# Band attention and two MLP layers on one core: the fourth f tile joins the banks of the first three, and batches 2 and 3 come first in the block products

## The chip, the core and the metric

The kernel runs on one core of a Trainium2 chip, in one launch. Its engines are TensorE (PE in the profile; PEld is its weight load), VectorE (DVE), ScalarE (ACT), GpSimd (POOL) and SyncE (SP), which here only issues DMAs. The metric is device time in microseconds, the median of several executions. One execution was profiled; all rows below come from it.

## What is computed

The reference, cut to what matters: attention over 4 batches, 8 heads, 512 local and 32 global tokens with 64 elements a head; then two MLP layers (512 to 2048 to 512) over all 2304 tokens.

```python
x = attn_out.transpose(0, 2, 1, 3).reshape(B * S, H * D)   # 2304 x 512
h = x @ w_in                                               # layer 0, 2048 wide
g = np.where(h > 0, h, np.exp(np.minimum(h, 0)) - 1)
x = g @ w_out
h = x @ w_in2                                              # layer 1
g = np.where(h >= 1, h, np.where(h <= -1, 0, (h + 1) ** 2 / 4))
return g @ w_out2
```

## The kernel before, in words

**Numbers.** Every fp32 operand of the MLP is held as two parts, high and low (`xh`, `xl`; `gh`, `gl`; a weight's two halves), and a product is three matmuls: low weight by high x, high by low, high by high. Weights arrive as 64-bit words in a `wraw` tile (two buffers) and are split by `decode`, which takes eight steps on DVE and two on ACT, most of them 128x1024.

**The two layers.** The hidden width of a layer is 16 f tiles of 128. The tokens are four batches j of 512 local tokens, plus one group of global rows. For an f tile and a batch, `up` makes 12 matmuls of 128x512 into one PSUM bank, ACT and DVE apply the function and split the result, and `down` makes 12 matmuls into four banks (dn0 to dn3, one for each 128 of the output). When the last f tile of a group is added, `collect` evicts each bank with ACT into an `ev` tile, which a DMA takes to `sums` in DRAM: a plain store by SP for the group that has f = 0, an accumulating DMA by POOL for the others. The `ev` tile is free again when that DMA is through. A `rows` item does the same for the global rows.

**Plain f tiles.** In layer 0 the f tiles 0 to 3 are done that way ("plain"): `PLAIN = [[0, 1, 2], [3]]`. The first three go over batches 0, 1, 2, 3 and are evicted. The fourth, whose weights `decode_one` brings, follows over batches 2, 3, 0, 1 as a group of its own, with its own evictions and its own `rows` item; its downs spread into what comes next.

**Block products.** All other f tiles go in 14 pairs by Strassen-Winograd blocks. A pair and a duo of batches (duo 0 is batches 0 and 1, duo 1 is 2 and 3) make seven products of 6 matmuls (`quad`, `product`), in place of the 8 blocks of plain products. Each takes a form of x (X11, X21, X22, T1 to T4). Forms are made by `first_forms` for layer 0 (and `later_forms` for layer 1), stored to `forms` in DRAM, and held in the tiles that had the tokens (`PLACES`). When the groups switch from one duo to the other, `product` issues two loads of 512 KB for each form once its last reader is under way (`load_form`). In the first group, duo 0, the three X forms stand where batches 0 and 1 have their tokens; the four T forms, made in spare tiles of `w_ps[0]` and stored, are loaded into the tiles of batches 2 and 3.

**What sets the order.** Code is written in events; after each event `pop` may emit one waiting down, and `step` advances the jobs in `line` (`decode_in`, `decode_out`, `first_forms`, ...), which `job_at` starts at an event number. A scheduler then orders the instructions of each engine by what is ready. Every engine works its own list in order. PE, for instance, can't pass a matmul that waits.

## Time and profile before

| | |
|---|---|
| median of 3 runs | 852.78 us (851.49 to 853.75) |
| the profiled execution | 852.66 us, span 850.9 us |
| granted TensorE clock, mean | 0.991 |
| PE busy | 814.0 us, 96% of the span |
| DVE busy | 685.6 us, 81% |
| ACT busy | 554.3 us, 65% |
| POOL busy | 102.3 us, 12% |
| DMA | 180.88 MB |

PE is nearly always at work, so the table alone says little; time is lost where a window of PE is not full. The attention ends about 115 to 128 us into the span, the plain f tiles and the first block products fill 120 to 260 us, and the switch from layer 0 to layer 1 lies around 460 to 540 us. In a window row the columns are busy microseconds of PE, PEld, DVE, ACT and POOL, then the granted clock as a share of the full one, the mean busy share of the 16 DMA engines, and GB/s.

### The profile page before, as it was taken

How to read it: one execution, taken by the hardware profiler on the slowest of the kernel's cores; microseconds unless marked ns; L12 is line 12 of the kernel's file. 1: busy time of each engine (PE TensorE's matmuls, PEld its weight loads, DVE VectorE, ACT ScalarE, POOL GpSimd, SP SyncE). 2: the span in 40 equal slices, each digit the busy share in tenths (PEclk: the TensorE clock that was granted, in tenths of full speed). 3: DMA queues.
4: the chain of work that ended last, by engine and by line, in shares of the span. 5: the costliest groups of instructions: out<-in, count | busy, mean ns of one | idle time of the engine just before them, and what ended most of it. 6: DMA issues, size and time to landing. Idle time of an engine off the chain costs nothing.

```text
span 850.9 us, 15914 instructions
## 1 busy us (share of the span) xinstructions
PE 814.0 (96%) x6058; PEld 662.6 (78%) x6058; DVE 685.6 (81%) x1279; ACT 554.3 (65%) x948; POOL 102.3 (12%) x162
## 2 busy tenths in 40 slices
PE   8799999998979999999999988999999999999998
PEld 5676778886758888888888866788888888888886
DVE  5798889968869979786789899998988598945463
ACT  5788765855746667555656366878867686867451
POOL 2231300002213022201100000000020111111000
PEclk9999999999999999999999999999999999999999
DMA  8988729997999189538916846437853795369523
GB/s 268 318 262 275 255 85 373 370 392 213 298 328 160 43 245 318 115 65 211 313 69 247 297 187 259 148 99 250 294 119 79 198 323 123 49 142 302 200 101 110
DMA packets 67132, 180.88 MB, mean 213 GB/s; under 512 B 9328, under 2 KB 9584, under 8 KB 65904
## 3 DMA queue, kind: packets, MB, share of 16 engines
q1 hardware_dynamic: 55248, 158.62, 53.8%
q0 software_dynamic: 11520, 20.98, 15.3%
q8 instruction: 48, 0.79, 0.4%
q10 hardware_dynamic: 288, 0.26, 0.1%
q14 instruction: 28, 0.23, 0.1%
HBM read 116.65 MB, written 63.18 MB: 211 GB/s over the span
## 4 chain that ended last, share of the span: by engine, by line
PE 76%; DMA 11%; DVE 7%; ACT 5%; issue 2%; POOL 0%; SPq 0%; ACTq 0%; DVEq 0%; POOLq 0%
PE dn L368 34%; PE up L1054 26%; DMA wraw<-in_w 5%; PE up L281 3%; PE dn L381 2%; DMA xh<-form 2%; PE s L146 2%; PE up L293 2%; DMA k_sb<-in_kT 1%; PE pt L146 1%; DMA sum<-ev 1%; PE up L146 1%; PE po L146 1%; ACT sn L146 1%; DVE xl L861 1%
## 5 line engine op out<-in xcount | busy, mean ns | idle before, releaser
L1054 PE MATMUL up<-xh,wi 128*128 128x512 f32 x784 | 264.5, 397 | 12.8 <-DMA xh<-form 3.9
L368 PE MATMUL dn<-gh,wo 128*128 128x512 f32 x608 | 184.6, 391 | 3.7 <-ACT ev L347 3.4
L1054 PEld LDWEIGHTS up<-xh,wi 128*128 128x128 f32 x784 | 149.9, 191 | 47.6 <-DVE u L861 4.9
L861 DVE TENSOR_TENSOR u<-up,u 128x512 f32<-128x512 f32 x196 | 131.7, 686 | 51.4 <-PE up L1054 43.2
L1054 PE MATMUL up<-xl,wi 128*128 128x512 f32 x392 | 155.0, 395 | 0.0
L352 POOL DMA_DIRECT2D sum<-ev x80 | 72.7, 1118 | 593.8 <-ACT ev L347 588.9
L368 PEld LDWEIGHTS dn<-gh,wo 128*128 128x128 f32 x608 | 113.5, 188 | 29.2 <-ACT ev L347 5.5
L368 PE MATMUL dn<-gl,wo 128*128 128x512 f32 x304 | 114.4, 390 | 0.4 <-DVE gl L334 0.4
L330 ACT ACTIVATE gh<-g 128x512 fp32r<-128x512 f32 x123 | 77.1, 628 | 53.1 <-DVE g L313 20.0
L334 DVE TENSOR_TENSOR gl<-g,gh 128x512 fp32r<-128x512 f32 x123 | 84.0, 686 | 13.0 <-ACT gh L330 11.8
L1054 PEld LDWEIGHTS up<-xl,wi 128*128 128x128 f32 x392 | 75.0, 191 | 14.9
L347 ACT ACTIVATE ev<-dn 128x512 f32<-128x512 f32 x110 | 61.7, 597 | 34.2 <-PE dn L368 19.6
L306 ACT ACTIVATE g<-u,half_sb 128x512 f32<-128x512 f32 x64 | 45.8, 720 | 48.2 <-DVE u L861 40.0
L368 PEld LDWEIGHTS dn<-gl,wo 128*128 128x128 f32 x304 | 57.0, 188 | 12.8 <-DVE gl L334 0.9
L368 PE MATMUL dn<-gh,xl 128*128 128x512 f32 x160 | 62.2, 392 | 2.6 <-ACT gh L330 2.5
L368 PE MATMUL dn<-gh,xh 128*128 128x512 f32 x160 | 62.3, 389 | 0.0
L315 DVE TENSOR_TENSOR g<-u,g 128x512 f32<-128x512 f32 x64 | 43.8, 686 | 20.9 <-ACT g L308 20.9
L368 PE MATMUL dn<-gl,xh 128*128 128x512 f32 x160 | 58.4, 389 | 0.0
L307 ACT ACTIVATE g<-g,one_sb 128x512 f32<-128x512 f32 x68 | 48.7, 720 | 1.4
L301 ACT ACTIVATE g<-u 128x512 f32<-128x512 f32 x48 | 30.1, 630 | 26.1 <-DVE u L861 22.4
L303 ACT ACTIVATE g<-g,one_sb 128x512 f32<-128x512 f32 (+1 forms) x64 | 45.6, 714 | 1.5
L308 ACT ACTIVATE g<-g 128x512 f32<-128x512 f32 x68 | 42.5, 627 | 1.1
(189 smaller groups left out, 1357.3 us busy)
## 6 DMA issues: line engine op xcount, KB each, us to landing
wraw<-in_w SPq DMA_DIRECT2D x56, 512.0 KB, 6.6
xh<-form SPq DMA_DIRECT2D x46, 512.0 KB, 9.6
xl<-form SPq DMA_DIRECT2D x46, 512.0 KB, 8.1
sum<-ev POOLq DMA_DIRECT2D x80, 256.0 KB, 8.4
v_sb<-in_vwin SPq DMA_DIRECT2D x64, 260.0 KB, 4.6
form<-xh SPq DMA_DIRECT2D x20, 512.0 KB, 4.6
form<-xl SPq DMA_DIRECT2D x20, 512.0 KB, 4.3
sum<-ev SPq DMA_DIRECT2D x32, 256.0 KB, 5.4
```

The source lines that it names most:

```text
L146: return lambda *args, **kw: tc.keep_in_program_order(fn(*args, **kw))
L303: eng.scalar.activation(self.g, self.g, AF.Relu, bias=one_sb, scale=-1.0)
L306: eng.scalar.activation(self.g, self.ps, AF.Relu, bias=half_sb, scale=-0.5)
L307: eng.scalar.activation(self.g, self.g, AF.Relu, bias=one_sb, scale=-1.0)
L315: eng.vector.tensor_tensor(g, self.ps, g, ALU.max)
L330: eng.scalar.activation(self.gh, self.g, AF.Copy)
L334: eng.vector.tensor_tensor(self.gl, self.g, self.gh.bitcast(F32), ALU.subtract)
L347: eng.scalar.activation(out, ps, AF.Copy)
L352: eng.gpsimd.dma_start(to, out, accum_op=ALU.add)
L368: eng.tensor.matmul(banks[d], w[:, d * P:(d + 1) * P], g, start=first and k == 0, stop=last and k == 2)
L861: return eng.vector.tensor_tensor(out, a, b, op)
L1054: eng.tensor.matmul(ps, w[:, a, col + k * P:col + (k + 1) * P], x[b][:, k * SL:(k + 1) * SL], start=k + t == 0, stop=k == 1 and t == 2,)
```

## The change

Five things are changed, and one follows from them.

1. All four plain f tiles form one group. Per batch they add into the same four banks, which are evicted once, through SP. The `rows` item is one as well.
2. The first block group is duo 1 (batches 2 and 3), and the order of the duos in all later groups is mirrored. `PLACES` is mirrored too.
3. `first_forms(1)` makes the T forms straight into the tiles of batches 0 and 1, after the last up product that reads them ((0, 3, 1) is born). The eight loads of T forms before the first group fall away.
4. `decode_in(0)` starts at event 3 (was 5), `first_forms(1)` at 5 (was 3), `decode_in(1)` at 8 (was 10), `decode_out(0)` at 10 (was 8).
5. `decode_out` turns its three places by one: pair 0's output weights go into the token tile (3, 0), which is free when batch 3's last up product is done.
6. At the end of layer 0 the first two sums (not the last two) use the spare tile.

Counted in the order of the program: PE 4782 instructions before and after; ACT 952 and 933; DVE 1281 and 1278; POOL 167 and 151 (accumulating DMAs 80 and 64); SP 375 and 367.

```diff
-PLAIN = [[0, 1, 2], [3]]
+EARLY, LATE = [0, 1, 2], 3
+PLAIN = EARLY + [LATE]
...
@@ decode_in(n)
         yield
+        while n == 2 and len(w_ps) < 2:
+            yield
         w = w_ps[n % 3 // 2].tile([P, 2, 8 * BLOCK], F32R, tag=f"wi{n % 3}", name="wi")
...
@@ decode_out(n)
-        i = (n + 1) % 3
+        i = (n + 2) % 3
...
-        while len(w_ps) < 2:
+        while n in (1, 2) and len(w_ps) < 2 or n == 0 and (0, LATE, 3) not in born:
             yield
...
-            w = [token_tile(1, 0, part) for part in range(2)]
+            w = [token_tile(3, 0, part) for part in range(2)]
...
-    PLACES = {X11: (0, 0), X21: (0, 1), X22: (1, 1), T2: (2, 0), T3: (2, 1), T1: (3, 0), T4: (3, 1)}
+    PLACES = {X11: (2, 0), X21: (2, 1), X22: (3, 1), T2: (0, 0), T3: (0, 1), T1: (1, 0), T4: (1, 1)}
...
@@ first_forms(duo)
-        for i, j, h in ((X11, j0, 0), (X21, j0, 1), (X22, j1, 1)):
-            keep([flat(x[j][h]) for x in (xh, xl)], (0, duo, i), last_low[0])
+        if duo == 0:
+            for i, j, h in ((X11, j0, 0), (X21, j0, 1), (X22, j1, 1)):
+                keep([flat(x[j][h]) for x in (xh, xl)], (0, duo, i), last_low[0])
...
+        while duo and (0, LATE, 1) not in born:
+            yield
         for i, pair in enumerate((((T2, x22), (T3, x12)), ((T1, x11), (T4, x21)))):
-
-            t = w_ps[0].tile([P, 2, 2, 2 * SL], F32R, tag=f"wi{i}", name="form")
+            if duo == 0:
+
+                t = w_ps[0].tile([P, 2, 2, 2 * SL], F32R, tag=f"wi{i}", name="form")
             for k, (form, src) in enumerate(pair):
-                split([t[:, k, part] for part in range(2)], src)
-                keep([t[:, k, part] for part in range(2)], (0, duo, form))
+                out = new_form(form) if duo else [t[:, k, part] for part in range(2)]
+                last_split[0] = split(out, src)
+                if duo:
+                    holds[form] = 0, 1
+                keep(out, (0, duo, form))
...
@@ pop()
-                if layer == 0 and j >= 2:
-                    if j == 2:
+                if layer == 0 and j < 2:
+                    if j == 0:
...
-    job_at(3, first_forms(1), False)
-    job_at(5, decode_in(0))
-    job_at(8, decode_out(0))
-    job_at(10, decode_in(1))
-    for i, js in enumerate(((0, 1, 2, 3), (2, 3, 0, 1))):
-        fs = PLAIN[i]
...
+    job_at(3, decode_in(0))
+    job_at(5, first_forms(1), False)
+    job_at(8, decode_in(1))
+    job_at(10, decode_out(0))
+    for j in range(B):
+        for f in PLAIN:
+            ds = range(KT // 2, KT) if j == 0 and f in EARLY else range(KT)
+            downs.append(["down", 0, PLAIN, j, f, ds])
...
+    begin, item = rows(0, PLAIN, [(0, 0), (0, LATE)])
+    downs.append(item)
+    ups = [(f, j) for j in range(B) for f in PLAIN if (0, f, j) not in born]
+    for f, j in ups[1:2] + ups[0:1] + ups[2:]:
+        need(lambda: (0, f) in w_in)
+        event(lambda: plain(0, f, j))
...
-    need(lambda: all((0, duo, i) in made_forms for duo in range(2) for i in range(7)))
-    for i in (T2, T3, T1, T4):
-        load_form(0, 0, i)
...
-    for c, duos in enumerate(((0, 1), (1, 0), (0, 1), (0, 1), (1, 0), (0, 1), (1, 0))):
+    for c, duos in enumerate(((1, 0), (0, 1), (1, 0), (1, 0), (0, 1), (1, 0), (0, 1))):
```

How the order moves, at three places. First PE. Before, the downs of the fourth f tile (`wo_3083`) stand among the block products (`wi_3382`), into banks of their own, dn_3609 and the next:

```order
L1054 MATMUL up_3831<-xh_3755,wi_3382 128x512
L368 MATMUL dn_3609<-gh_3449,wo_3083 128x512 x2
L368 MATMUL dn_3609<-gl_3451,wo_3083 128x512
L1054 MATMUL up_3839<-xh_3759,wi_3382 128x512
L1054 MATMUL up_3839<-xl_3760,wi_3382 128x512
L1054 MATMUL up_3839<-xh_3759,wi_3382 128x512 x2
L1054 MATMUL up_3839<-xl_3760,wi_3382 128x512
L1054 MATMUL up_3839<-xh_3759,wi_3382 128x512
L368 MATMUL dn_3616<-gh_3449,wo_3083 128x512 x2
L368 MATMUL dn_3616<-gl_3451,wo_3083 128x512
L368 MATMUL dn_3623<-gh_3449,wo_3083 128x512 x2
L368 MATMUL dn_3623<-gl_3451,wo_3083 128x512
```

After, at the place where batch 0's first three f tiles end, some up products (`up_3325`), then the fourth tile's downs (`wo_3077`) into the banks dn_2979 to dn_3073 that batch 0 had, and then batch 1's first (dn_3216):

```order
L282 MATMUL up_3325<-xl_94,wh0_143 128x512
L282 MATMUL up_3325<-xh_92,wh0_143 128x512
L369 MATMUL dn_2979<-gh_3114,wo_3077 128x512 x2
L369 MATMUL dn_2983<-gh_3114,wo_3077 128x512 x2
L369 MATMUL dn_3069<-gh_3114,wo_3077 128x512 x2
L369 MATMUL dn_3073<-gh_3114,wo_3077 128x512 x2
L369 MATMUL dn_2979<-gl_3116,wo_3077 128x512
L369 MATMUL dn_2983<-gl_3116,wo_3077 128x512
L369 MATMUL dn_3069<-gl_3116,wo_3077 128x512
L369 MATMUL dn_3073<-gl_3116,wo_3077 128x512
L369 MATMUL dn_3216<-gh_2476,wl0_144 128x512
L369 MATMUL dn_3216<-gh_2476,wh0_143 128x512
```

The downs of the fourth tile have moved out of the block products to the end of each batch, and the next batch's downs follow them directly.

Second DVE, around the decode of the second pair's up weights. Before, `wi_3689` comes behind the output weights of the first pair (`wo_3576`):

```order
L239 SCALAR_TENSOR_TENSOR wo_3576<-rest_3578,wraw_3485 128x1024
L216 TENSOR_SCALAR rest_3691<-wraw_3637 128x1024
L220 SCALAR_TENSOR_TENSOR rest_3691<-wraw_3637,rest_3691 128x1024
L228 TENSOR_SCALAR top_3690<-top_3690 128x1024
L232 TENSOR_SCALAR top_3690<-top_3690 128x1024
L233 SCALAR_TENSOR_TENSOR top_3690<-wraw_3637,top_3690 128x1024
L238 TENSOR_SCALAR wraw_3637<-top_3690 128x1024
L239 SCALAR_TENSOR_TENSOR wi_3689<-rest_3691,wraw_3637 128x1024
L861 TENSOR_TENSOR whole_3746<-wi_3689 128x1024
L861 TENSOR_TENSOR mixed_3747<-whole_3746 128x256 x2
L861 TENSOR_TENSOR mixed_3747<-mixed_3747,whole_3746 128x256
L861 TENSOR_TENSOR mixed_3747<-whole_3746,mixed_3747 128x256
```

After, the second pair's weights are `wi_3557`:

```order
L240 SCALAR_TENSOR_TENSOR wi_3557<-rest_3559,wraw_3517 128x1024
L335 TENSOR_TENSOR gl_3515<-g_3509,gh_3513 128x512
L314 SCALAR_TENSOR_TENSOR g_3549<-up_3536,g_3549 128x512
L862 TENSOR_TENSOR whole_3602<-wi_3557 128x1024
L335 TENSOR_TENSOR gl_3555<-g_3549,gh_3553 128x512
L862 TENSOR_TENSOR mixed_3603<-whole_3602 128x256 x2
L314 SCALAR_TENSOR_TENSOR g_3594<-up_3581,g_3594 128x512
L862 TENSOR_TENSOR mixed_3603<-mixed_3603,whole_3602 128x256
L862 TENSOR_TENSOR mixed_3603<-whole_3602,mixed_3603 128x256
L335 TENSOR_TENSOR gl_3600<-g_3594,gh_3598 128x512
L862 TENSOR_TENSOR wi_3557<-mixed_3603,wi_3557 128x1024
L217 TENSOR_SCALAR rest_3658<-wraw_3611 128x1024
```

They stand among the last plain f tiles' work (`g`, `gl`), and the output weights of the first pair (xl_3656) come behind them.

Third SP, between the attention and the first block products. Before (`form_0_*` and `form_1_*` are the forms of duo 0 and 1 of layer 0, `wraw` weights):

```order
L958 DMA form_1_3_125<-form 128x1024
L1027 DMA xh<-form_0_2_117 128x1024
L958 DMA form_1_5_127<-form 128x1024
L958 DMA form_1_3_125<-form 128x1024
L1027 DMA xl<-form_0_2_117 128x1024
L1027 DMA xh<-form_0_4_119 128x1024
L1027 DMA xl<-form_0_4_119 128x1024
L958 DMA form_1_5_127<-form 128x1024
L350 DMA sum_2_109<-ev 128x512 x2
L867 DMA wraw<-in_w 128x512
L350 DMA sum_2_109<-ev 128x512 x2
L867 DMA wraw<-in_w 128x512
```

After:

```order
L961 DMA form_1_1_123<-xl 128x1024
L961 DMA form_1_5_127<-xl 128x1024
L868 DMA wraw<-in_w 128x512 x2
L961 DMA form_1_6_128<-xh 128x1024
L961 DMA form_1_6_128<-xl 128x1024
L868 DMA wraw<-in_w 128x512 x2
L351 DMA sum_3_110<-ev 128x512 x4
L868 DMA wraw<-in_w 128x512 x2
L1037 DMA xl<-form_0_0_115 128x1024
L1037 DMA xh<-form_0_0_115 128x1024
L1037 DMA xl<-form_0_1_116 128x1024
L1037 DMA xh<-form_0_1_116 128x1024
```

The loads `xh<-form` and `xl<-form` ahead of the weights are gone; the first ones now belong to the first switch of duos.

## Rows read from the trace of the kernel before

**Rows 1.** The page, busy time, share of the span and instructions of each engine

```profile
PE 814.0 (96%) x6058; PEld 662.6 (78%) x6058; DVE 685.6 (81%) x1279; ACT 554.3 (65%) x948; POOL 102.3 (12%) x162
```

**Rows 2.** Windows: width, busy PE, PEld, DVE, ACT, POOL, clock, DMA share, GB/s

```profile
120.00:140.00 20.00, 19.87 (x148) 15.77 (x148) 18.14 (x26) 10.61 (x20) 0.00 (x0) 1.00 0.57 216
140.00:160.00 20.00, 20.00 (x90) 16.57 (x89) 19.18 (x23) 14.79 (x25) 0.00 (x0) 1.00 1.01 380
160.00:180.00 20.00, 20.00 (x94) 16.87 (x93) 17.97 (x25) 13.86 (x21) 0.00 (x0) 1.00 1.02 391
180.00:200.00 20.00, 20.00 (x96) 16.66 (x95) 12.66 (x19) 12.00 (x21) 0.00 (x0) 1.00 0.87 328
200.00:220.00 20.00, 15.16 (x57) 11.19 (x56) 16.66 (x23) 11.47 (x19) 7.88 (x8) 0.91 0.89 224
220.00:240.00 20.00, 16.11 (x81) 13.21 (x80) 18.97 (x29) 14.58 (x23) 6.05 (x7) 0.97 1.08 307
240.00:260.00 20.00, 18.68 (x76) 14.70 (x75) 12.67 (x19) 9.88 (x17) 4.82 (x5) 0.94 0.96 279
260.00:280.00 20.00, 20.00 (x91) 16.48 (x91) 19.96 (x30) 13.12 (x20) 3.54 (x4) 1.00 0.89 188
```

**Rows 3.** Timeline of PE, 200 to 262 us: start, length, instruction, [idle before, its releaser]

```profile
202.28 0.72 PE L368 MATMUL dn<-gh,wo 128*128 128x512 f32 x2 [1.22 <-ACT ev L347]
...
203.08 0.62 PE L368 MATMUL dn<-gh,wo 128*128 128x512 f32 x2
...
203.77 0.62 PE L368 MATMUL dn<-gh,wo 128*128 128x512 f32 x2
...
208.22 0.80 PE L1054 MATMUL up<-xh,wi 128*128 128x512 f32 x1 [2.90 <-DVE wi L239]
...
211.72 0.62 PE L1054 MATMUL up<-xh,wi 128*128 128x512 f32 x2
...
215.57 0.73 PE L368 MATMUL dn<-gh,wo 128*128 128x512 f32 x2 [0.72 <-ACT ev L347]
...
239.36 0.77 PE L1054 MATMUL up<-xh,wi 128*128 128x512 f32 x1 [3.89 <-DMA xh<-form]
...
242.06 0.76 PE L368 MATMUL dn<-gh,wo 128*128 128x512 f32 x2
...
249.02 0.50 PE L368 MATMUL dn<-gh,xl 128*128 128x512 f32 x1 [0.49 <-ACT gh L330]
...
254.90 0.73 PE L368 MATMUL dn<-gh,wo 128*128 128x512 f32 x2 [0.82 <-ACT ev L347]
```

**Rows 4.** Windows of 2 us, the same columns

```profile
208.00:210.00 2.00, 1.78 (x4) 1.50 (x5) 1.86 (x4) 0.45 (x1) 0.00 (x0) 0.55 1.10 196
...
240.00:242.00 2.00, 2.00 (x6) 1.58 (x5) 1.86 (x3) 0.61 (x2) 0.86 (x1) 0.50 1.06 293
```

**Rows 5.** The chain of waits from 195 to 262 us: start, length, what

```profile
204.93 9.92 DMA sum<-ev
...
221.02 18.21 DMA xh<-form
```

**Rows 6.** Timeline of DVE: the fourth f tile's weights, the second pair's up weights

```profile
130.32 1.23 DVE L239 SCALAR_TENSOR_TENSOR wo<-rest,wraw 128x1024 fp32r<-128x1024 uint32 x1
...
206.94 1.22 DVE L239 SCALAR_TENSOR_TENSOR wi<-rest,wraw 128x1024 fp32r<-128x1024 uint32 x1
```

**Rows 7.** DMA issues of 200 to 262 us: count, KB each, median us to landing

```profile
sum<-ev POOLq DMA_DIRECT2D x20, 256.0 KB, 8.6
...
xh<-form SPq DMA_DIRECT2D x7, 512.0 KB, 17.6
```

**Rows 8.** DMA issues of 128 to 200 us

```profile
xh<-form SPq DMA_DIRECT2D x4, 512.0 KB, 8.1
```

**Rows 9.** Groups of ACT's instructions from 124 to 280 us: busy, mean ns, idle before

```profile
L347 ACT ACTIVATE ev<-dn 128x512 f32<-128x512 f32 x38 | 21.7, 598 | 17.1 <-DMA sum<-ev 7.6 <-PE dn L368 7.4 <-PE up L1054 1.9
```

**Rows 10.** A window of 20 us at the layer switch, columns as in group 2

```profile
500.00:520.00 20.00, 16.93 (x70) 13.35 (x71) 20.00 (x26) 11.55 (x16) 0.00 (x0) 0.83 0.46 184
```

**Rows 11.** Timeline of SP at the layer switch

```profile
474.85 15.98 SPq L867 DMA_DIRECT2D wraw<-in_w  x4
```

More of the change, by code (lines that the diff above doesn't have):

```diff
@@ L40 @@
 NB = B + 1
-PLAIN = [[0, 1, 2], [3]]
+EARLY, LATE = [0, 1, 2], 3
+PLAIN = EARLY + [LATE]
 WCOLS = KT * P + DM
-W_EARLY = len(PLAIN[0])
+W_EARLY = len(EARLY)
 UP_EARLY = 5
@@ L186, in band_attention_then_two_mlps @@
     rows_in[0, 0] = lambda k, part: early[part][:, :, k * P:(k + 1) * P]
-    for f in PLAIN[0]:
+    for f in EARLY:
         w_in[0, f] = [w[:, f, 0:KT * P] for w in early]
@@ L753, in early_ups @@
         def early_ups():
-            for f, j in [(f, j) for j in range(B) for f in PLAIN[0]][:UP_EARLY]:
+            for f, j in [(f, j) for j in range(B) for f in EARLY][:UP_EARLY]:
                 u = Up(0, f, j)
@@ L836, in band_attention_then_two_mlps @@
                 ps_dn.append(mpool("ps_dn0", 1, space=PSUM))
-                for f in PLAIN[0]:
-                    down(0, PLAIN[0], 0, f, first, range(KT // 2))
+                for f in EARLY:
+                    down(0, PLAIN, 0, f, first, range(KT // 2))
         for _ in weights:
@@ L878, in decode_one @@
             pass
-        rows_in[0, 1] = lambda k, part: w[:, part, k * P:(k + 1) * P].rearrange("p (f c) -> p f c", f=1)
+        rows_in[0, LATE] = lambda k, part: w[:, part, k * P:(k + 1) * P].rearrange("p (f c) -> p f c", f=1)
         w_in[0, f] = [w[:, i, 0:KT * P] for i in range(2)]
@@ L1034, in band_attention_then_two_mlps @@
     banks = {0: first}
-    born = {(0, f, j): -LAG for f, j in [(f, j) for j in range(B) for f in PLAIN[0]][:UP_EARLY]}
+    born = {(0, f, j): -LAG for f, j in [(f, j) for j in range(B) for f in EARLY][:UP_EARLY]}
     made_forms, holds, summed, w_out_uses = set(), {}, {}, {}
@@ L1199, in event @@
             pop()
+        if len(w_ps) < 2 and not any(PLAIN in item for item in downs):
+            w_ctx.close()
+            w_ps.append(mpool("w_third", 1))
         for fn in soon.pop(now[0], []):
@@ L1212, in job_at @@
         due.setdefault(n, []).append((job, ahead))
-    job_at(0, decode_one(PLAIN[1][0]))
+    job_at(0, decode_one(LATE))
     job_at(1, first_forms(0), False)
-    job_at(3, first_forms(1), False)
-    job_at(5, decode_in(0))
-    job_at(8, decode_out(0))
-    job_at(10, decode_in(1))
-    for i, js in enumerate(((0, 1, 2, 3), (2, 3, 0, 1))):
-        fs = PLAIN[i]
-        for j in js:
-            for f in fs:
-                ds = range(KT // 2, KT) if i + j == 0 else range(KT)
-                downs.append(["down", 0, fs, j, f, ds])
-        begin, item = rows(0, fs, [(0, i)])
-        downs.append(item)
-        for j in js:
-            for f in fs:
-                if (0, f, j) not in born:
-                    if i:
-                        need(lambda: (0, f) in w_in)
-                    event(lambda: plain(0, f, j))
-            if len(w_ps) < 2 and i:
-                while downs[0][2 if downs[0][0] == "down" else 4] == PLAIN[0]:
-                    pop()
-                w_ctx.close()
-                w_ps.append(mpool("w_third", 1))
-        event(begin)
@@ L1241, in band_attention_then_two_mlps @@
-    for i, (j, h) in ((X11, (0, 0)), (X21, (0, 1)), (X22, (1, 1))):
+    job_at(3, decode_in(0))
[6 more added lines that the diff above has]
+            downs.append(["down", 0, PLAIN, j, f, ds])
+    last_split = [None]
+    begin, item = rows(0, PLAIN, [(0, 0), (0, LATE)])
+    downs.append(item)
+    ups = [(f, j) for j in range(B) for f in PLAIN if (0, f, j) not in born]
@@ L1242, in band_attention_then_two_mlps @@
+    for f, j in ups[1:2] + ups[0:1] + ups[2:]:
+        need(lambda: (0, f) in w_in)
+        event(lambda: plain(0, f, j))
+        if ready():
+            pop()
+    event(begin)
+    for i, (j, h) in ((X11, (2, 0)), (X21, (2, 1)), (X22, (3, 1))):
         slot[i] = [flat(x[j][h]) for x in (xh, xl)]
-        holds[i] = 0, 0
-    need(lambda: all((0, duo, i) in made_forms for duo in range(2) for i in range(7)))
-    for i in (T2, T3, T1, T4):
-        load_form(0, 0, i)
+        holds[i] = 0, 1
+        keep(slot[i], (0, 1, i), last_split[0])
@@ L1257, in band_attention_then_two_mlps @@
             if c == 3:
-                job_at(at + 2, later_forms(1), False)
+                job_at(at + 2, later_forms(0), False)
             job_at(at + 5 + late, decode_in(2 * c + 2))
@@ L1261, in band_attention_then_two_mlps @@
             if c == 2:
-                job_at(at + 9, later_forms(0), False)
+                job_at(at + 9, later_forms(1), False)
             job_at(at + 12 + late // 3, decode_in(2 * c + 3))
```

## The prediction

> **What bounds the kernel now.** I read the page first: TensorE (PE) is busy in 814.0 of the span's 850.9 us [rows 1], so only time that PE loses can be won, and the question is where it loses. The windows of 20 us answer it: from 120 to 200 us, and again from 260 us on, PE is at 19.87 to 20.00 of 20; it falls to 15.16, 16.11 and 18.68 between 200 and 260 [rows 2]. That is the stretch in which the fourth f tile, called [3] here, and the first block products run, and it is what the diff rewrites. PE's own timeline there shows six holes: 1.22, 2.90, 0.72, 3.89, 0.49 and 0.82 us, together 10.04 [rows 3]; the reader should look at the bracket behind each row, which names what ended the hole. After the two longest, the granted clock is at its half level (0.55 and 0.50 in the windows of 2 us) [rows 4]. What that costs comes from the spacing: at the full level three matmuls take 203.77 − 203.08 = 0.69 us, 0.23 each; from 208.22 to 211.72 stand 8 matmuls where 8 × 0.23 = 1.84 would do (1.66 lost), from 239.36 to 242.06 stand 6 where 1.38 would do (1.32 lost) [rows 3]. So the stretch loses 10.04 + 2.98 = 13.0 us. The causes, hole by hole:
>
> - 1.22, 0.72 and 0.82 us end with an eviction on ACT. The chain of waits shows why the second is late: an accumulating DMA of POOL is in flight for 9.92 us from 204.93 on, and the next eviction needs its `ev` tile back [rows 5]. These are the evictions of [3] and of the first blocks' downs.
> - 2.90 us ends with the DVE instruction that writes `wi` of the second pair (206.94, 1.22 us long) [rows 6]. DVE was not slow, it was given decode_in(1) last of all.
> - 3.89 us ends with the load of a form: issued at 221.02, landed 18.21 us later [rows 5].
> - 0.49 us ends with an ACT copy; I leave it where it is.
>
> **The change part by part.**
>
> *One set of evictions.* 16 of 38 ACT evictions of the stretch 124 to 280 us [rows 9] and 16 accumulating DMAs of POOL fall away, since [3] adds into the banks of the first three. Their ACT time (16 × 0.598 = 9.6 us) and DMA time lie beside PE; on the path stood only the holes of 1.22 and 0.72 us, at [3]'s banks. Both go: −1.94. The 0.82 us hole is at a group that stays; I count half: −0.4.
>
> *The same matmuls, in another place.* No matmul is added or dropped (4782 before and after in the program's order). PE's work until the end of the first block products is the same, so the end of the plain stage moves by what it waits, not by what it does. Moved in front: 12 up and 12 down matmuls per batch of [3], whose weights DVE finishes at 131.55 (130.32 and 1.23 us) [rows 6]; PE comes to them at about 132.1, counted in matmuls of 0.23 us from 120 us on, so no wait there; were the decode late, the nearest hole of that kind, 2.90, bounds the price.
>
> *A new wait.* All downs of a batch now end on the same four banks, and the next batch's first down follows at once on PE (the order shows dn_3216 right behind the last of dn_2979 to dn_3073). It waits for the evictions, which on ACT can sit behind one 128x1024 `top` that itself waits for a weight load. Behind the waiting matmul PE's queue is in order, so nothing passes it. The trace of before has no such row at this place; bounds from the nearest: 0 (before, the same handover between batches inside [0, 1, 2] cost nothing: PE 20.00 in 160 to 200 [rows 2]) and the 2.90 of [rows 3] with its 1.66 for the clock. I take +0.6 for the first handover and +0.8 for the three others together, since ACT has 4 evictions of 0.598 us and PE needs the first bank after one of them.
>
> *decode_in(0) and decode_in(1) earlier, decode_out(0) later.* The order puts wi_3557 (second pair) ahead of the first block products. Walking DVE's queue with the durations of the trace from 131.5 us, it is done at about 192, while PE comes to the second pair at about 204: 12 us of room, and the hole of 2.90 with its 1.66 goes: −4.56. In exchange decode_out(0) goes behind it, into tile (3,0), which is free only after the last up product of batch 3; by the same walk it is written at 203 to 205 and its first reader stands on PE at about 206. Nothing covers a slip there; price 0 to 2.90, taken +0.5.
>
> *Forms of duo 1 straight into tiles.* Eight loads of 512 KB are gone and eight stores read from the token tiles instead of `form` tiles; the 8 split operations on DVE and ACT are the same. They wait for (0, 3, 1) to be born, about 140 us; behind them on DVE stands decode_in(1), which has the 12 us above. SP's queue keeps the stores in the same stretch, where the DMA share is already 1.01 to 1.02 without a loss on PE (20.00) [rows 2].
>
> *The first switch of duos.* The X11 load of before took 18.21 us because it shared the DMA engines with the accumulates: in 200 to 262 us the median of a load of `xh` is 17.6 us beside 20 POOL transfers, while in 128 to 200 us, without them, it is 8.1 [rows 7, 8]. After the change, the load of X11 is issued at about 205 and T3's at about 218 by the walk, needed at 221 and 234.5; POOL's first accumulate comes at about 240. With some 7 MB to move at the 307 GB/s of 220 to 240 us [rows 2] the last lands near 226: some 8 us to spare, so the 3.89 and its 1.32 go: −5.21. If the loads still took 18.21 us, T3's would land at 236.2, 1.7 late.
>
> *The rest.* In the groups behind, the two duos change names and the order stays. The switch of layers at 480 to 540 us (PE 16.93 in 500 to 520 at a clock of 0.83 [rows 10]) is mirrored, with a few stores in other places: ±3 by the size of one hole there, taken 0.
>
> Sum against the profiled execution, 852.66 us (span 850.9 and 1.8 around it; the median of the runs, 852.78, is 0.12 away): 852.66 − 1.94 − 0.4 − 4.56 − 5.21 + 0.6 + 0.8 + 0.5 = 842.45. Taking the 0.49 too would give 842.0. I say **842.4**.
>
> **The rivals.**
>
> *B, DVE becomes the bound.* DVE is busy 18.14 + 19.18 + 17.97 + 12.66 + 16.66 + 18.97 + 12.67 = 116.25 of the 140 us from 120 to 260 [rows 2]. With 12 us taken out, the same work must fit into 128, a share of 0.91. For it: the room is small. Against it: from 260 to 280 DVE is at 19.96 of 20 while PE is at 20.00, so a full DVE does not by itself stop PE. If DVE's waits for PE and ACT hold it at 0.88, it takes 132.1 us, 4 more: 846.5.
>
> *C, one set of banks.* Each handover of banks idles as the 1.22 us hole does, in all four batches, 4.9 us instead of the 1.4 taken, and the clock falls once more (+1.3): 847.2. For it: the new wait above. Against it: before, the same kind of handover left PE at 20.00.
>
> The Trainium skill (TensorE: Matmul & The Clock Gate, section "A second HAM failure mode: psum-queue depth-cycling") reports a kernel whose cycling through PSUM banks gives short idles between groups of matmuls, and a clock that swings between its levels. That is this rival's rule, and it speaks against the change; by the trace of before (clock 1.00 in 160 to 200 us over two such handovers) it does not act here so far.
>
> *D, the loads at the first switch are still late.* Nothing of the 5.21 is won: 847.7.
>
> *E, slower.* At the switch of layers SP spends 15.98 us on issuing four weight loads, at 474.85, because their buffers come free late [rows 11]; the `sums` loads and the form stores ahead of them change places. If the weights of the first pair of layer 1 slip by as much again behind the new stores, with layer 0's products already used up on PE, that is +16: 858.4. It decides once the slip is over the 10 us that the earlier part gained; below that the kernel is still faster.
>
> *F, the gain is not there.* The plain stage's end is not set by what I named, and the time won before 260 is waited away at the next late operand: 852.7.
>
> **How the numbers follow.** Forecast 0.58; B 0.16; C 0.08; D 0.08; E 0.04; F 0.06. The likeliest gives 842.4, with 839 to 845.5 by its own bounds (nothing lost at the handovers, 0.49 and the whole 0.82 won: 840; less 1 from the layer switch; the upper ends of the new waits: +3). B, C and D end at 847.7, so the range goes from 838.8 to 848.2; E and F lie outside. A measurement of this kernel can tell 0.3% (2.6 us) from no change: faster than 850.2 is all of the forecast, B, C and D and a little of F, 0.88; within, 0.07; slower, 0.05.
>
> **What would show it.** Right: in the trace after, no hole over 1 us on PE between 200 and 250 us, no half-level window there, the chain of waits without a form load in it, no POOL accumulate before about 235 us. Right for the new wait: `dn` rows with a short idle behind "ACT ev" near 148 us. Wrong: DVE at 20.00 in every window from 200 to 260 with PE waiting for `u` or `gl` (B); a row of idle at every batch's first `dn` (C); a load of X11 or T3 ending a hole (D); the windows 480 to 540 much below 17 (E).

## The result and the profile after

The changed kernel takes 840.08 us (median of 4 runs, 838.48 to 840.94), against 852.13 us for the kernel before on the same chip; the ratio is 0.9855 with a 95% interval of 0.9832 to 0.9878, so 12 us or 1.4% faster. The forecast was 842.4 us, with a range of 838.8 to 848.2. The profiled execution took 840.41 us, its span is 838.6 us.

The windows of 20 us, with the columns of [rows 2] (width, busy PE, PEld, DVE, ACT, POOL, granted clock, DMA share, GB/s):

```profile
140.00:160.00 20.00, 19.99 (x88) 16.26 (x87) 20.00 (x26) 15.76 (x24) 0.00 (x0) 1.00 0.89 327
160.00:180.00 20.00, 20.00 (x90) 16.55 (x89) 18.49 (x23) 12.60 (x18) 0.00 (x0) 1.00 0.65 242
180.00:200.00 20.00, 20.00 (x98) 17.03 (x97) 15.96 (x22) 10.56 (x18) 0.00 (x0) 1.00 1.02 359
200.00:220.00 20.00, 20.00 (x92) 16.54 (x91) 18.82 (x26) 13.48 (x21) 0.00 (x0) 1.00 0.80 265
220.00:240.00 20.00, 20.00 (x101) 17.03 (x100) 19.21 (x31) 11.79 (x18) 0.00 (x0) 1.00 0.93 343
240.00:260.00 20.00, 19.99 (x90) 16.21 (x90) 17.98 (x25) 14.61 (x23) 7.63 (x8) 1.00 0.77 130
```

PE had 15.16, 16.11 and 18.68 busy us in the three windows from 200 to 260 us [rows 2]; it now has 20.00, 20.00 and 19.99, and the clock stays at 1.00. PE's timeline lists no hole from 130 to 470 us, where before it listed the six of [rows 3]. POOL, which began its accumulating transfers at 202.55 us, now begins at 242.97:

```profile
242.97 3.74 POOL L353 DMA_DIRECT2D sum<-ev  x4 [133.19 <-ACT ev L348]
```

The loads of forms, 17.6 us in the median in 200 to 262 us before [rows 7], take 8.0. The issues of that stretch after (count, KB, median us to landing):

```profile
wraw<-in_w SPq DMA_DIRECT2D x8, 512.0 KB, 6.5
xl<-form SPq DMA_DIRECT2D x7, 512.0 KB, 7.1
xh<-form SPq DMA_DIRECT2D x7, 512.0 KB, 8.0
sum<-ev POOLq DMA_DIRECT2D x8, 256.0 KB, 6.9
```

The switch of layers is not better. PE's holes there, in the timeline after:

```profile
477.60 0.47 PE L369 MATMUL dn<-gh,xl 128*128 128x512 f32 x1 [1.10 <-DVE sums L356]
...
489.43 0.58 PE L294 MATMUL up<-wi,xh 128*128 128x256 f32 x1 [3.62 <-DVE u L862]
...
508.98 0.74 PE L369 MATMUL dn<-gh,wo 128*128 128x512 f32 x2 [1.21 <-DVE wo L240]
```

From 440 to 540 us PE idled 8.74 us before (busy 91.26 of 100); in the 100 us from 428 on it now idles 9.46 (busy 90.54). The granted clock is 0.97 over these 100 us in both, so half-level stretches cost some 3 us in each (an estimate from the clock).

**How runs are compared below.** All programs here have the same list of PE instructions up to the last transposes of the attention (`ot`), yet the time of that row differs from profile to profile:

```profile
130.00 0.60 PE L147 MATMUL ot<-eye_sb,o_sb 128*128 128x128 f32 x4
```

```profile
126.33 0.60 PE L147 MATMUL ot<-eye_sb,o_sb 128*128 128x128 f32 x4
```

These are the changed kernel and one of the experiments (i_scalar_q); the kernel before stands at 127.67, and b_in1_first at 130.79. So up to 4.5 us of a total come from a stage that no edit touches. Each kernel has one profile, so whether such a difference belongs to the kernel or to the run is not shown. I therefore also give the length from that row to the end of the span: 850.9 − 127.67 = 723.2 us before, 838.6 − 130.00 = 708.6 after. By that measure the change is worth 14.6 us; the medians say 12.

### The profile page after: what moved, and what is told of

Its sections match the earlier page's. It is cut to its first block, busy times and chain, and to the rows that moved or that the text cites. A ratio compares the mean times of both kernels' runs of the same rounds, so it can differ in the third digit from the quotient of the medians.

```text
span 838.6 us, 15816 instructions
## 1 busy us (share of the span) xinstructions
PE 809.2 (96%) x6058; PEld 661.8 (79%) x6058; DVE 685.6 (82%) x1276; ACT 547.4 (65%) x929; POOL 87.6 (10%) x146
## 4 chain that ended last, share of the span: by engine, by line
PE 83%; DVE 7%; DMA 4%; ACT 3%; issue 3%; SPq 0%; DVEq 0%
PE dn L369 38%; PE up L1064 28%; PE up L282 4%; PE up L294 3%; DMA wraw<-in_w 3%; PE dn L382 2%; PE s L147 2%; PE up L147 1%; PE po L147 1%; DVE u L862 1%; PE pt L147 1%; DVE xl L862 1%; ACT sn L147 1%; ACT pT L147 1%; PE ot L147 1%
## 5 line engine op out<-in xcount | busy, mean ns | idle before, releaser
L1064 PE MATMUL up<-xh,wi 128*128 128x512 f32 x784 | 258.6, 391 | 1.8 <-DVE u L862 1.0
L369 PE MATMUL dn<-gh,wo 128*128 128x512 f32 x608 | 180.4, 390 | 2.9 <-ACT gh L331 1.7
L1064 PEld LDWEIGHTS up<-xh,wi 128*128 128x128 f32 x784 | 147.3, 188 | 33.8 <-DVE u L862 1.9
L1064 PE MATMUL up<-xl,wi 128*128 128x512 f32 x392 | 152.7, 389 | 0.0
L353 POOL DMA_DIRECT2D sum<-ev x64 | 58.4, 1250 | 594.6 <-ACT ev L348 593.7
L369 PE MATMUL dn<-gl,wo 128*128 128x512 f32 x304 | 110.7, 389 | 0.0
L369 PEld LDWEIGHTS dn<-gl,wo 128*128 128x128 f32 x304 | 57.1, 188 | 11.9
L348 ACT ACTIVATE ev<-dn 128x512 f32<-128x512 f32 x96 | 53.4, 599 | 19.3 <-PE dn L369 18.0
L316 DVE TENSOR_TENSOR g<-u,g 128x512 f32<-128x512 f32 x64 | 43.6, 685 | 14.6 <-ACT g L309 14.5
L302 ACT ACTIVATE g<-u 128x512 f32<-128x512 f32 x48 | 30.2, 629 | 35.8 <-DVE u L862 29.4
L308 ACT ACTIVATE g<-g,one_sb 128x512 f32<-128x512 f32 x68 | 48.7, 721 | 1.3
L304 ACT ACTIVATE g<-g,one_sb 128x512 f32<-128x512 f32 x63 | 45.5, 723 | 1.5
```

Of the source, the lines that this page charges most:

```text
L304: eng.scalar.activation(self.g, self.g, AF.Relu, bias=one_sb, scale=-1.0)
L308: eng.scalar.activation(self.g, self.g, AF.Relu, bias=one_sb, scale=-1.0)
L316: eng.vector.tensor_tensor(g, self.ps, g, ALU.max)
L348: eng.scalar.activation(out, ps, AF.Copy)
L353: eng.gpsimd.dma_start(to, out, accum_op=ALU.add)
L369: eng.tensor.matmul(banks[d], w[:, d * P:(d + 1) * P], g, start=first and k == 0, stop=last and k == 2)
```

## The experiments

Each kernel is told with its edit, what was expected, and what came. "Length" is from the `ot` row to the end. The theory at the start was the prediction's: six holes with causes of their own, of which one is the late decode. Its rivals were that the mirrored duos with their saved loads are the gain, or that the accumulating transfers are behind all of it.

**m_old_duos: one set of banks, but batches 0 and 1 first.**

```diff
-    PLACES = {X11: (2, 0), X21: (2, 1), X22: (3, 1), T2: (0, 0), T3: (0, 1), T1: (1, 0), T4: (1, 1)}
+    PLACES = {X11: (0, 0), X21: (0, 1), X22: (1, 1), T2: (2, 0), T3: (2, 1), T1: (3, 0), T4: (3, 1)}
...
+    need(lambda: all((0, duo, i) in made_forms for duo in range(2) for i in range(7)))
+    for i in (T2, T3, T1, T4):
+        load_form(0, 0, i)
```

> The changed kernel with batches 0 and 1 first again, their T forms made in spare tiles, stored, and loaded back (eight loads of 512 KB) before the first block products; the four plain f tiles still share one set of banks and decode_in(1) is still ahead of decode_out(0). Theory (one set of banks takes away the 16 accumulating transfers, and with the early decode that is nearly all of the gain; the mirrored duos are only a convenience): 840 to 843 us, no hole over 1 us between 130 and 260 us except perhaps at the load of T1 or T4, whose tiles of batch 3 come free last. Rival (the loads that the mirrored duos save are the gain): 848 to 852 us, with a hole of 3 to 6 us at a form load before the first block products.

842.79 us, ratio 0.9858 (0.9821 to 0.9895), length 710.7. PE's only hole from 128 to 290 us is 1.22 us, at 235.51, behind a decode. Six sevenths of the gain (12.5 of 14.6 us) come without the mirrored duos and with the eight loads back in. The rival that the saved loads are the gain falls.

**a_own_group: everything else of the change, but the fourth f tile a group of its own.**

```diff
-            downs.append(["down", 0, PLAIN, j, f, ds])
+    for fs in (EARLY, [LATE]):
...
+                downs.append(["down", 0, fs, j, f, ds])
```

> The changed kernel with the fourth f tile as a group of its own again: its up and down products follow those of the first three over batches 0 to 3, with its own 16 evictions and 16 accumulating transfers of POOL; duos mirrored, forms made straight into tiles, decode_in(1) early, as in the changed kernel. Theory (the second set of evictions and the accumulates are a cause of their own): holes at evictions come back (1.2 to 2.8 us with what a hole costs on top), and form loads of the first switch take 14 us or more, with 0 to 5.5 us of PE waiting for one: 843 to 848 us. Rival (the mirrored duos and the decode order alone bring the gain): 839 to 841.5 us, no hole over 0.5 us between 200 and 255.

854.35 us, ratio 0.9989 (0.9968 to 1.0011), length 724.8: nothing of the gain is left, more loss than the 843 to 848 us expected. PE's holes between 200 and 250 us add up to 11.0 us, most of them behind an eviction. Two of the seven:

```profile
207.59 0.50 PE L1064 MATMUL up<-xh,wi 128*128 128x512 f32 x1 [2.09 <-DVE u L862]
...
235.07 0.50 PE L369 MATMUL dn<-gh,xl 128*128 128x512 f32 x1 [3.12 <-ACT ev L348]
```

The mirrored duos, the direct forms and the early decode are worth nothing together as long as the second set of evictions and its transfers are there.

**b_in1_first: the kernel before, decode_in(1) ahead of decode_out(0).**

```diff
-    job_at(8, decode_out(0))
-    job_at(10, decode_in(1))
+    job_at(8, decode_in(1))
+    job_at(10, decode_out(0))
```

> The kernel before with one edit: decode_in(1) is started at event 8 and decode_out(0) at event 10 (they change places). Theory (each hole has a cause of its own and PE carries a won microsecond on): the 2.90 us hole goes with its half-level stretch (1.66) and about 0.27 us that a hole costs on top of its idle time, 4.8 in all, so 847.5 us, unless the first downs then wait for decode_out(0), which would give back 1 to 3. The hole of 3.89 at the form load stays, or grows, since the load is asked for earlier by as much as PE is. Rival (the next late operand swallows what is won, the accumulating transfers bound the stretch): 851 to 853 us, the form-load hole grown to 7 us or more.

862.29 us, ratio 1.0091 (1.0065 to 1.0116), length 727.6: slower than before, which neither side expected. By medians that is 8 us, by length 4.4. The hole at `wi` shrinks from 2.90 to 0.45, as the theory has it; but in place of the 3.89 at a form load there are now two such holes, and a third one, much larger, ends with an eviction:

```profile
229.92 0.47 PE L1054 MATMUL up<-xh,wi 128*128 128x512 f32 x1 [2.12 <-DMA xh<-form]
...
235.16 0.59 PE L1054 MATMUL up<-xh,wi 128*128 128x512 f32 x1 [3.62 <-DMA xh<-form]
...
249.48 1.22 PE L368 MATMUL dn<-gh,wo 128*128 128x512 f32 x2 [8.35 <-ACT ev L347]
```

The block products of the second pair now come before most downs of the fourth tile, so PE asks for the forms earlier, and the accumulates come later. The chain of waits names what stands behind the 8.35:

```profile
229.80 17.90 DMA wraw<-in_w
...
247.80 0.04 ACT top L213
...
248.85 0.59 ACT ev L347
```

A weight load takes 17.90 us in that crowd, a decode step on ACT waits for it, and the eviction waits behind that step. An earlier decode alone is a loss.

**b_no_acc: the kernel before without the 16 accumulating transfers.**

```diff
+            if fs == PLAIN[1]:
+                return
             to = sums[layer + 1, j][:, d, :]
```

> The kernel before without the 16 accumulating DMAs of the fourth f tile: its 16 evictions on ACT stay, but what they write goes nowhere, so the fourth f tile's part of the sums is left out. Theory (the loads at the first switch are late because POOL's accumulating transfers share the DMA engines with them, and the evictions because their ev tile waits for such a transfer): the holes of 1.22, 0.72, 0.82 and 3.89 us go or shrink under 0.5, with the half-level stretch behind the 3.89; the 2.90 at the decode stays: 843 to 845 us, median landing of a form load in 200 to 240 us 8 to 10 us in place of 17.6. Rival (the loads are late because of their own 7 MB behind the weights on SP's queue): the 3.89 stays, 848 to 850 us, landing still over 14 us.

841.32 us, ratio 0.9854 (0.9808 to 0.9899), length 711.2. PE's holes from 200 to 290 us are three:

```profile
203.49 0.73 PE L370 MATMUL dn<-gh,wo 128*128 128x512 f32 x2 [1.21 <-ACT ev L347]
...
208.89 0.73 PE L370 MATMUL dn<-gh,wo 128*128 128x512 f32 x2 [0.35 <-ACT ev L347]
...
243.84 0.73 PE L370 MATMUL dn<-gh,wo 128*128 128x512 f32 x2 [0.28 <-ACT ev L347]
```

The time is below the 843 to 845 us expected, and two holes did not do what was expected of them. The form load's 3.89 is gone, as it should be. But the 1.22 at the first eviction, which was to go or to fall under 0.5, is still there with 1.21, so no accumulating transfer caused it. The chain of waits has a decode step of ACT ahead of that eviction:

```profile
201.82 1.14 ACT top L213
202.96 0.49 ACT ev L347
```

And the 2.90 at `wi`, which was expected to stay, is gone, although DVE writes `wi` no earlier than before: it is done 80.4 us behind the `ot` row, against 80.5 before (206.94 and 1.22 in [rows 6]).

```profile
208.02 1.23 DVE L239 SCALAR_TENSOR_TENSOR wi<-rest,wraw 128x1024 fp32r<-128x1024 uint32 x1
```

The order of PE says why: ahead of the second pair's first product its list now holds eight groups of the fourth tile's downs (dn_3657 to dn_3785, three matmuls each) where before it held four (dn_3661 to dn_3682). The scheduler had put the other four behind that product, since their evictions were to wait for a transfer: b_acc_no_wait, below, where the transfers are there and the wait is not, has eight as well. Twelve matmuls of 0.23 us are 2.8 us of cover.

**a_out0_first: the changed kernel with the old order of the two decodes.**

```diff
-    job_at(8, decode_in(1))
-    job_at(10, decode_out(0))
+    job_at(8, decode_out(0))
+    job_at(10, decode_in(1))
```

> The changed kernel with decode_out(0) at event 8 and decode_in(1) at event 10, the old order of these two. By the prediction's step (the early decode of the second pair takes the 2.90 us hole away) the hole comes back, larger, since the decode of the second pair now waits for the tile (3, 0) as well: 845 to 848 us. By the rival that the first experiments suggest (that hole came from the downs that the accumulates kept out of PE's list, not from the decode): 839 to 842 us, hole under 0.5.

839.89 us, ratio 0.9815 (0.975 to 0.988), length 708.3, the same as the changed kernel, and PE has no hole from 130 to 290 us. The exchange of the two decodes is worth nothing. It doesn't follow that the time of the decode is. Measured from the `ot` row, which in this run stands at 130.71, 3 us later than in the kernel before, `wi` of the second pair is done after 76.6 us here and after 80.5 before, since the first pair's `wi`, whose decode starts at event 3 here too, is done after 29.4 us in place of 48.9. The first pair's and the second pair's `wi` on DVE, and PE's first product of the second pair:

```profile
158.94 1.21 DVE L240 SCALAR_TENSOR_TENSOR wi<-rest,wraw 128x1024 fp32r<-128x1024 uint32 x1
...
206.13 1.22 DVE L240 SCALAR_TENSOR_TENSOR wi<-rest,wraw 128x1024 fp32r<-128x1024 uint32 x1
```

```profile
208.09 0.40 PE L1064 MATMUL up<-xh,wi 128*128 128x512 f32 x1
```

The kernel before has the first pair's here:

```profile
175.35 1.22 DVE L239 SCALAR_TENSOR_TENSOR wi<-rest,wraw 128x1024 fp32r<-128x1024 uint32 x1
```

PE comes to that product 77.4 us behind the row (77.7 before, at the start of its hole), 0.7 us after `wi` is done. So the time fits the rival, but its reason does not show here: the decode is no longer late.

**b_acc_no_wait: the transfers stay, but no eviction waits for one.** Each of the 16 reads a tile that is not written there.

```diff
+                acc = eng.gpsimd.dma_start(
+                    to, xh[GR].rearrange("p k n -> p (k n)").bitcast(F32), accum_op=ALU.add
+                )
```

> The kernel before, with the 16 accumulating DMAs of the fourth f tile kept in number, size and place, but reading a tile that nobody writes in this stretch in place of the ev tile (what is added to the sums is wrong, so the fourth f tile's part of the output is); each still starts behind its eviction, but no eviction waits for one. Theory A (the accumulates cost through ACT: its eviction waits for the ev tile, and PE's banks and the downs behind it): 841 to 844 us, as without the transfers, holes at evictions under 1.3 in all. Theory B (they cost through the DMA engines that they share with the form loads): the form load still ends a hole of 2 to 4 us and takes 14 us or more to land, 845 to 849 us.

850.83 us, ratio 0.995 (0.9922 to 0.9978), length 719.4. PE's order has the same eight groups of downs as b_no_acc, the `wi` hole is gone as there, and the two holes that come in its place are both ended by a form load:

```profile
204.27 0.73 PE L373 MATMUL dn<-gh,wo 128*128 128x512 f32 x2 [1.20 <-ACT ev L347]
...
209.69 0.73 PE L373 MATMUL dn<-gh,wo 128*128 128x512 f32 x2 [0.37 <-ACT ev L347]
...
242.32 0.77 PE L1059 MATMUL up<-xh,wi 128*128 128x512 f32 x1 [3.58 <-DMA xh<-form]
...
247.41 0.47 PE L1059 MATMUL up<-xh,wi 128*128 128x512 f32 x1 [2.19 <-DMA xh<-form]
```

The loads' landing in 200 to 262 us:

```profile
sum<-xh POOLq DMA_DIRECT2D x16, 256.0 KB, 17.0
xl<-form SPq DMA_DIRECT2D x7, 512.0 KB, 17.4
xh<-form SPq DMA_DIRECT2D x7, 512.0 KB, 18.2
```

The mechanism is theory B's, the time above its 845 to 849 us. Against b_no_acc, which has the same order of PE until behind these holes, the transfers alone cost 8.2 us of length (719.4 against 711.2), though nothing waits for them but the DMA engines.

**b_plain_store and b_pool_store: the same bytes without the adding.** The 16 evictions go as plain stores to another place, by SP in the one and by POOL (`eng.gpsimd` in the line below) in the other.

```diff
+            if fs == PLAIN[1]:
+                eng.sync.dma_start(sums[0, j][:, d, :], out)
```

> The kernel before, with the 16 evictions of the fourth f tile sent by SP as plain stores of the same size to another place in DRAM, in place of POOL's accumulating DMAs (the fourth f tile's part of the sums is left out). The same bytes leave, and each eviction still waits for its ev tile. Theory (an accumulating DMA holds the DMA engines about twice as long for a byte as a plain one: in 200 to 262 us of the kernel before, POOL's 4.97 MB make 46.5% of the engines' time and SP's 11.54 MB 51.5%): a form load lands in 8 to 12 us, the hole of 3.89 us at the first switch goes or falls under 1.5, 842 to 847 us. Rival (any 4.2 MB more beside the loads delay them as much): landing over 14 us, the form-load hole stays over 3 us, 849 to 853 us.

844.26 us, ratio 0.9904 (0.9876 to 0.9931), length 714.3; a load of `xh` lands in 7.7 us, and no load ends a hole. PE's holes from 200 to 290 us are 1.20, 2.80 and 0.89, the second at `wi` with the old order of PE.

> The kernel before, with the 16 evictions of the fourth f tile sent by POOL as plain stores to another place in DRAM (the fourth f tile's part of the sums is left out): same queue and bytes as before, no adding. With SP's plain stores the time was 844.26 us. Theory (the adding itself costs: the DMA engines read the old sums and write them back): 842 to 847 us, the form-load hole of 3.89 gone, POOL's queue under 7% of the DMA engines' time for a MB. Rival (POOL's queue costs, adding or not): 849 to 853 us, the hole stays over 3 us, POOL's queue near 9% for a MB as before.

845.42 us, ratio 0.9893 (0.9855 to 0.9932), length 714.7; a load of `xh` lands in 13.5 us, and none ends a hole. So it is the adding, not POOL's queue and not the bytes, that costs most: 723.2 with adding, 714.3 to 714.7 with stores, 711.2 with nothing. The DMA queues in 200 to 262 us (packets, MB, share of the 16 engines; q0 is POOL's) of the kernel before:

```profile
q1 hardware_dynamic: 3168, 11.54, 51.5%
q0 software_dynamic: 2723, 4.97, 46.5%
```

and of b_pool_store:

```profile
q1 hardware_dynamic: 3456, 12.58, 56.9%
q0 software_dynamic: 1897, 5.33, 30.4%
```

Before, a MB takes 46.5 / 4.97 = 9.4% on POOL's queue and 51.5 / 11.54 = 4.5% on SP's. With 16 of POOL's 24 transfers plain, and the other 8 still adding, its share is 30.4 / 5.33 = 5.7%.

**a_two_evictions: two evictions in each batch, the accumulates early.**

```diff
-            downs.append(["down", 0, PLAIN, j, f, ds])
+            downs.append(["down", 0, EARLY if f in EARLY else [LATE], j, f, ds])
```

> The changed kernel, all up and down products in its order, but the four banks are evicted twice in each batch: behind the first three f tiles (through SP) and behind the fourth (16 accumulating DMAs of POOL, now between 145 and 205 us, beside the form stores). Theory (what costs is accumulates beside the block products and the loads of the first switch): 840 to 844 us, no hole over 1.3 us, POOL idle from 210 to 235 us. Rival (each second eviction and accumulate costs wherever it stands): 846 to 853 us, with holes at dn rows all through 145 to 205 us.

846.89 us, ratio 0.9899 (0.9843 to 0.9955), length 716.6: in the rival's range, but the holes are neither side's. The early accumulates cost next to nothing (one hole of 0.67 us at 149.77), as the theory says. At the end of the plain stage, though, an eviction ends a hole of 4.36 us, where the theory had none over 1.3, and the clock falls to 0.50 behind it:

```profile
204.28 1.22 PE L369 MATMUL dn<-gh,wo 128*128 128x512 f32 x2 [4.36 <-ACT ev L348]
```

The chain of waits has that eviction behind a decode step of ACT, and the step behind a weight load:

```profile
189.71 12.79 DMA wraw<-in_w
```

Why that load took so long is not shown; POOL issued accumulates beside it, from 186.60 to 192.26 us. So the place of the accumulates matters; whether their number does as well, this run can't tell.

**i_scalar_q, i_pool_forms, i_pool_forms_q: the switch of layers.** Three attempts at what is left. The first loads the first layer-1 pair's weights by ACT's queue:

```diff
+        raw = words(KT * P, [(w1, w2)[layer][f][:, 0:KT * P] for f in fs], eng.scalar if n == 6 else None)
```

> The changed kernel, with one edit at the switch of layers: the two loads of the first layer-1 pair's up weights are issued by ACT in place of SP. In the changed kernel the load is issued at 455.73 us, right behind 14 form stores on the same queue, lands 15.76 us later, and DVE waits 4.24 us for it. Theory (a second queue is served beside the first one, not behind it): landing in 6 to 10 us, DVE's wait gone, the 3.62 us hole of PE at 489 shorter by as much, 835 to 838 us. Rival (the engines are full there, the queue makes no difference; or DVE is the bound anyway): 839.5 to 841 us.

838.98 us, ratio 0.981 (0.9751 to 0.987), length 708.0, between the two forecasts and by length the same as the changed kernel. DVE's wait for these weights falls from 4.24 to 3.3 us only, and the hole of 3.62 us is there again, at 484.78, as the rival has it. The second gives DVE's work on the forms to POOL:

```diff
+            if i in (T1, T4, X22):
...
+                eng.gpsimd.tensor_tensor(lo, src, hi.bitcast(F32), ALU.subtract)
...
-        add(x11, x12, x11, ALU.subtract)
...
+        eng.gpsimd.tensor_tensor(x11, x12, x11, ALU.subtract)
```

> The changed kernel; at the switch of layers, the four adds of each duo's layer-1 forms and the low parts of its forms T1, T4 and X22 (128x1024 each) go to POOL in place of DVE, 14 instructions that cost DVE some 1.13 us each. Theory (DVE is the bound from 480 to 520 us, where PE idles 9.5 us in 460 to 540): DVE gets 8 us or more of room behind 470 us, PE's hole of 3.62 at 489 falls under 1.5, 834 to 838 us. Rival (POOL takes so long for them, or slows DVE so much, that forms come late): 840 us or more, DVE's instructions of 128x1024 longer than 1.22 us beside POOL's.

> The same with the two loads of the first layer-1 pair's up weights issued by ACT in place of SP. Alone that edit changed little (838.98 against 840.08 us, span from the attention's end 708.0 against 708.6). Theory (with DVE relieved, the wait for these weights is what is late next): 2 to 4 us less than the kernel with POOL's share alone. Rival (it still is not): within 1 us of it.

846.40 us (ratio 0.9927, 0.9901 to 0.9954) and 847.24 us (0.994, 0.9919 to 0.9961), lengths 715.3 and 716.7: 6 to 8 us worse than the changed kernel, the rival in both. POOL takes 2.6 to 3.4 us where DVE takes 1.22, and it holds DVE up. Timeline of POOL, then of DVE, in i_pool_forms:

```profile
436.95 2.72 POOL L1028 TENSOR_TENSOR sum<-sum 128x1024 f32<-128x1024 f32 x1 [42.22 <-DVE xl L862]
439.75 3.26 POOL L1029 TENSOR_TENSOR sum<-sum 128x1024 f32<-128x1024 f32 x1
```

```profile
435.60 1.22 DVE L862 TENSOR_TENSOR xl<-sum,xh 128x1024 fp32r<-128x1024 f32 x1
...
437.33 0.68 DVE L862 TENSOR_TENSOR u<-up,u 128x512 f32<-128x512 f32 x1
437.93 2.82 DVE L862 TENSOR_TENSOR xl<-sum,xh 128x1024 fp32r<-128x1024 f32 x1
440.68 2.88 DVE L314 SCALAR_TENSOR_TENSOR g<-u,g 128x512 f32<-128x512 f32 x1
443.48 0.68 DVE L862 TENSOR_TENSOR u<-up,u 128x512 f32<-128x512 f32 x1
```

DVE's `xl` (1.22 us alone, as at 435.60) and `g` (0.68 alone) last 2.82 and 2.88 us beside POOL, `u`, which reads PSUM, stays at 0.68. The Trainium skill (SBUF — State Buffer, section "SBUF: two separate sides") says that DVE with two SBUF inputs and a GpSimd instruction that reads SBUF share one port pair under a lock held for the whole instruction; the rows agree.

## Why the prediction was right, and where its steps were not

*The total.* 842.4 was forecast, 840.41 came in the profiled run and 840.08 in the median, inside the range. The place was right: all of the gain lies between 130 and 260 us.

*The size of the loss.* I counted 13.0 us. Taking every matmul there at 0.227 us leaves 15.1: besides its idle time each of the six holes costs some 0.27 us, in the row ahead of it and in its own. For the first one: 202.28 − 200.68 − 1.22 = 0.38 for one matmul, and two matmuls from 202.28 take until 202.85, 0.57 in place of 0.46. The rows of the kernel before on both sides of [rows 3]'s first:

```profile
200.68 0.39 PE L1054 MATMUL up<-xh,wi 128*128 128x512 f32 x1
...
202.85 0.40 PE L368 MATMUL dn<-gl,wo 128*128 128x512 f32 x1
```

With the holes gone that went too; the 2.3 us by which the attention was longer in that run, and the switch, came off again.

*One set of evictions.* Right, but far too small as a term: −2.34 was put down for the eviction holes, while with the second set and its transfers back nothing of the gain is left (a_own_group). The 0.82 us hole, counted by half, went whole, and the 0.49, counted not at all, went too: 0.9 us more. That the evictions wait for the transfers is true of the 0.72, which shrinks to 0.35 to 0.37 where no eviction waits (b_no_acc, b_acc_no_wait); the 1.22 stays at 1.20 or 1.21 in all four kernels without the waits or the adding, so it is not theirs: a decode step stands ahead of that eviction on ACT (b_no_acc).

*The first switch of duos, −5.21.* Right in mechanism, too small in size: the accumulates share the DMA engines with the loads, and b_acc_no_wait against b_no_acc puts that at 8.2 us. The walk was right at its ends and not between: the first load was issued at 208.30 (about 205 was forecast) and POOL began at 242.97 (about 240), but the last load was issued at 230.45 and landed 7.2 us later, where the walk had it landed near 226. No load ended a hole all the same.

*The decode order, −4.56.* The hole went, and the mechanism of the step is what the trace shows: `wi` of the second pair is done at 187.19 (about 192 was forecast), and PE comes to it with the second matmul of the row at 206.73, at about 207 (about 204):

```profile
185.96 1.23 DVE L240 SCALAR_TENSOR_TENSOR wi<-rest,wraw 128x1024 fp32r<-128x1024 uint32 x1
```

```profile
206.73 0.62 PE L1064 MATMUL up<-xh,wi 128*128 128x512 f32 x2
```

What failed is the term as a summand of its own. First, an earlier decode alone shrinks the hole and makes the kernel 4.4 us longer (b_in1_first), since the next late operands take more than it gave. Second, in the kernel before the hole came as much from PE's list as from DVE: the transfers also set where the scheduler put the downs, and with twelve matmuls more ahead the same late decode makes no hole (b_no_acc). Third, the exchange of the two decodes, a part of the step, is worth nothing (a_out0_first): with the first pair's decode early, the hole is gone without it. But in the changed kernel PE's list has only three matmuls more than before ahead of that product. With `wi` done as far behind the `ot` row as before, 80.5 us, it would come at 210.5, some 3.5 us behind PE (an estimate from these rows). So the earlier decode seems to be needed there; no run has the changed kernel with both decodes as late as before, and what the term is worth in it stays open.

*The new waits, +0.6, +0.8, +0.5.* None came: PE is at 19.84 to 20.00 in every window, and no `dn` row has a hole. These 1.9 us are nearly the whole error of 2.0 against the profiled run, but partly by chance: the 0.9 of the two holes and the 2.1 by which the loss was counted too small would have put the time lower still, and the attention stage, 2.3 longer in that run, and the switch, 0.7 longer, put it back.

*The rivals.* B: DVE is at 18.82, 19.21 and 17.98 of 20 in the three windows from 200 us, and PE doesn't wait; the room was small and enough. C did not happen, and the Trainium skill's rule on cycling through PSUM banks (TensorE: Matmul & The Clock Gate, section "A second HAM failure mode: psum-queue depth-cycling") did not act: the clock was 1.00 in every window from 120 to 260 us. D did not happen. E: the switch of layers lost 0.7 us more idle time, within the ±3.

*The mirrored duos and direct forms* were given no term, and are worth about 2 us of length (708.6 against 710.7), one hole with what it costs, not apart from noise in the medians.

## What to carry to other kernels

When PE waits in several places for several engines, look for one stream that all of these share before giving each hole a cause. Here 16 accumulating DMAs of 256 KB stood behind a late load, some of the late evictions and, through the static order of the instructions, the missing cover for a late decode. A hole that is closed alone can cost time, when PE then comes too early to the next operand (b_in1_first). And before an operand is called as late as before, its time is to be taken from a mark that all runs share: in a_out0_first `wi` is within 1 us of the old time counted from the start of the span, and 3.9 us earlier counted from the `ot` row. If partial sums can stay in PSUM for one more term, that is worth more than the eviction's own time, above all just ahead of loads that have a deadline.

## What was not expected of the hardware

- A MB of accumulating DMA took about twice the DMA engines' time of a plain MB (9.4% against 4.5% of 62 us). In the changed kernel the 8 accumulates that are left in 200 to 262 us took more, 22.1 / 1.85 = 11.9% for a MB:

```profile
q0 software_dynamic: 1006, 1.85, 22.1%
```

- POOL instructions on SBUF stretched DVE's to their own length (2.82 and 2.88 in place of 1.22 and 0.68 us).
- A hole of 2.80 us on PE in b_plain_store left the granted clock at 1.00 in its window, one of 2.90 in the kernel before was followed by 0.55. What decides stays open.
- The attention stage, with the same PE list, ended between 126.33 and 130.79 us. Where single microseconds are compared, the stretch behind it is the better measure.
